# The second MLP of a three-stage kernel in three groups of 768 tokens, one PSUM bank a block, with norm sums in one column, a halved last tile and a wait margin on transfers

## The chip, the core and the metric

One core of a Trainium2 chip runs the whole program in one launch. The metric is device time in microseconds (us), the median of the runs of a kernel. The engines are TensorE (PE in the profile), VectorE (DVE), ScalarE (ACT), GpSimd (POOL) and SyncE (SP), which only issues transfers here.

## The reference

Three stages, in fp32; q, k and v of the attention are fp32, the weights come as float64 and are converted on the chip.

```python
def _attn_ref(q, k, v, phi):               # batch 4, heads 8, seq 576, head_dim 64, n_mem 32
    a = phi - np.max(phi, axis=2, keepdims=True)
    a = np.exp(a)
    a = a / (np.sum(a, axis=2, keepdims=True) + 1e-09)
    k_m = np.einsum('bhsm,bhsd->bhmd', a, k)
    v_m = np.einsum('bhsm,bhsd->bhmd', a, v)
    ...                                     # softmax(scale * q @ k_m.T) @ v_m
def _moe_ref(x, w_in, w_out):              # 2304 tokens, 512 -> 2048 -> 512
    h = x @ w_in
    g = h * (1.0 / (1.0 + np.exp(-1.702 * h)))
    return (g @ w_out).astype(np.float32)
def _moe2_ref(x, w_gate, w_val, w_out, rms_g):   # 2304 tokens, 512 -> 1536 -> 512
    rms = np.sqrt(np.mean(x * x, axis=-1, keepdims=True) + 1e-06)
    xn = x / rms * rms_g
    g = xn @ w_gate
    silu = g * (1.0 / (1.0 + np.exp(-g)))
    val = xn @ w_val
    return (silu * val @ w_out).astype(np.float32)
```

## The kernel before, in words

**Numbers.** A product of fp32 values is made of three matmuls of fp32r parts: each operand is split into a high part (a cast on ACT) and a low part (a subtraction on VectorE or POOL; function `split`), and high x high, low x high and high x low are summed in PSUM.

**Stages.** Attention works by batch and half of the heads; its output feeds the first MLP (steps `a_g1`, `a_g2`), which runs over two pairs of batches, 1152 tokens each, and eight groups of 256 hidden units, and adds into the tiles `x2_0` and `x2_1`. Meanwhile the weights of the second MLP are loaded, converted from float64 (`w_conv c ...`, tiles `raw_c`, `cv`) and put into a DRAM cache.

**The second MLP, the stage of the change.** First RMS norm, by 384 tokens: `norm_1` squares and adds (tiles `sq`, `sr`), `norm_2` sums over the partitions by matmuls against ones into `pnm` and takes the inverse root on columns of 3 (tile `r`), `norm_3` spreads it by transposes (`pnr`, `rb`), `norm_4` scales `x2`. Then gate and value products by a Winograd-like scheme: tokens form two halves, hidden units and inputs two blocks each, and 7 products (weights A11, A12, S1 to S4, A22 against token blocks B11, B21, B22, T1 to T4) stand for 8. The token blocks are made by `t_a` to `t_d` in big tiles `tba`, `tbb`, `tbc`, `tbd`. For each of 12 groups f of 128 hidden units, `s_g3` runs the products (`product`, line 1496) and collects them in tiles `c`, named p, u, v and s: ACT copies a product out of PSUM, VectorE adds the next one to it (`c<-c,ps_S`), ACT applies silu, and the two results are multiplied and split into `pp` tiles. After every second f, `s_g4` multiplies by the output weights (512 columns, PSUM tile `pg4`) and adds into `oacc`; `put` sends finished rows from SP.

The pass runs twice: "b" for the first pair of batches, "s" for the second. In "b" the weight blocks (`s0_f_...`, in the profile `s_A`, `s_S`, `s_o`) are made from the cached weights (`s_weights`, tile `s`, `raw_b_vg`) and written to `cache_s`; "s" reads them back (`s_again`). In "b" also the last conversions and the norm of the second pair are done.

A product here has 576 tokens and takes two PSUM banks, 288 columns in each:

```python
for q in range(2):
    n = slice(q * HALF, q * HALF + HALF)
    for y, z in ((0, 0), (1, 0), (0, 1)):
        for e in range(2):
            PE.matmul(ps[:, 512 * q : 512 * q + HALF], lhsT=a[y][:, e], rhs=b[:, z, e, n], ...)
```

**What orders the work.** Every operation is recorded first (all of them by the helper at line 612) and then ordered by `Plan.order`, a list scheduler with costs for each operation, due times (`dues`), a table that makes steps due earlier (`HASTE`) and a table that moves single operations to another engine (`OTHER`). Where PE would find no work before an operation that takes a new PSUM tile, `fill` puts matmuls on the constant `ones_r` there. Each engine and the SP queue then run their instructions in that fixed order. PSUM is a pool of 4 tiles of two banks each, `big` has 6 tiles, `cv` 5, `w` 10, `gp` 3.

## Time and profile before

| | before |
|---|---|
| median of 3 runs | 834.79 us (833.22 to 837.85) |
| the profiled execution | 838.53 us, of it span 836.8 us |
| PE busy | 820.4 us (98%) |
| VectorE busy | 630.9 us (75%) |
| ACT busy | 439.1 us (52%) |
| POOL busy | 223.2 us (27%) |
| moved by DMA | 166.92 MB, 199 GB/s |
| mean granted clock | 0.996 |

The span is from the first to the last instruction; 1.7 us of the execution lie outside it. Busy shares are over the whole span; since the stages have different limits, the table by stage tells more. In a row, "out<-in xcount" names the tile written and those read (buffer numbers left out), and a "releaser" is what ended a wait. A matmul's own duration overlaps with its neighbours, so the pace is read from starts, not from durations. In the profile tiles are grouped by the first part of their names, so `ps_A` stands for `ps_A11` and `ps_A12`, `pg` also for `pg4`. The second MLP runs from 409 to 832.

### The profile page before, as it was taken

How to read it: one execution, taken by the hardware profiler on the slowest of the kernel's cores; microseconds unless marked ns; L12 is line 12 of the kernel's file. 1: busy time of each engine (PE TensorE's matmuls, PEld its weight loads, DVE VectorE, ACT ScalarE, POOL GpSimd, SP SyncE). 2: the span in 40 equal slices, each digit the busy share in tenths (PEclk: the TensorE clock that was granted, in tenths of full speed). 3: DMA queues.
4: the chain of work that ended last, by engine and by line, in shares of the span. 5: the costliest groups of instructions: out<-in, count | busy, mean ns of one | idle time of the engine just before them, and what ended most of it. 6: DMA issues, size and time to landing. Idle time of an engine off the chain costs nothing.

```text
span 836.8 us, 15257 instructions
## 1 busy us (share of the span) xinstructions
PE 820.4 (98%) x5893; PEld 784.2 (94%) x5893; DVE 630.9 (75%) x1052; ACT 439.1 (52%) x774; POOL 223.2 (27%) x187
## 2 busy tenths in 40 slices
PE   8899999899999999999999999999999999999997
PEld 7799999899999999999999999999999999999996
DVE  7889999799899899899898788576775334445444
ACT  5797766577688565655566545444352332222220
POOL 4533384434542433682511112122000000000000
PEclk9999999999999999999999999999999999999999
DMA  9996756957967975564776579263556452633504
GB/s 340 286 289 159 256 175 214 221 174 260 287 205 225 325 217 191 197 207 152 242 244 226 177 248 333 111 239 122 169 170 193 155 176 73 206 120 108 176 1 113
DMA packets 76759, 166.92 MB, mean 199 GB/s; under 512 B 7312, under 2 KB 29328, under 8 KB 76688
## 3 DMA queue, kind: packets, MB, share of 16 engines
q1 hardware_dynamic: 76688, 165.97, 61.3%
q8 instruction: 46, 0.75, 0.4%
q14 instruction: 25, 0.20, 0.1%
HBM read 106.69 MB, written 59.24 MB: 198 GB/s over the span
## 4 chain that ended last, share of the span: by engine, by line
PE 89%; DVE 3%; DMA 2%; ACT 1%; issue 1%; SPq 0%; DVEq 0%
PE pg L612 50%; PE ps_A L612 23%; PE ps_S L612 9%; PE pq L612 2%; PE pvm L612 2%; DMA stage<-in_v_dram 2%; PE pk L612 1%; DVE pad L612 1%; DVE x L612 1%; PE pnm L612 0%; DVE stage L612 0%; DVE gr L612 0%; PE pnr L612 0%; DVE vm_0l L612 0%; DVE vm_1l L612 0%
## 5 line engine op out<-in xcount | busy, mean ns | idle before, releaser
L612 PE MATMUL pg<-gr,a_outh 128*128 128x384 f32 (+1 forms) x736 | 193.6, 334 | 0.0
L612 PEld LDWEIGHTS pg<-gr,a_outh 128*128 128x128 f32 x736 | 132.8, 188 | 0.6 <-DVE gr L612 0.3
L612 PE MATMUL pg<-gr,a_outl 128*128 128x384 f32 (+1 forms) x368 | 121.9, 331 | 0.0
L612 PE MATMUL pg<-s_o,pp 128*128 128x512 f32 x432 | 112.6, 390 | 0.0
L612 ACT COPY c<-ps_A 128x576 f32<-128x576 f32 x72 | 46.1, 641 | 115.4 <-PE ps_A L612 114.4
L612 PEld LDWEIGHTS pg<-s_o,pp 128*128 128x128 f32 x432 | 79.5, 188 | 15.0
L612 DVE TENSOR_TENSOR x<-x,pg 128x768 f32<-128x768 f32 (+1 forms) x86 | 80.0, 930 | 17.3 <-PE pg L612 16.2
L612 DVE TENSOR_TENSOR oacc<-oacc,pg 128x1024 f32<-128x1024 f32 (+1 forms) x54 | 56.3, 1042 | 47.2 <-PE pg L612 47.0
L612 PE MATMUL ps_A<-tba,s_A 128*128 128x288 f32 x576 | 83.1, 295 | 0.0
L612 PEld LDWEIGHTS ps_A<-tba,s_A 128*128 128x128 f32 x576 | 79.1, 188 | 0.8
L612 POOL TENSOR_TENSOR gr<-gf,gr 128x192 fp32r<-128x192 f32 (+2 forms) x47 | 49.6, 1063 | 88.3 <-ACT gr L612 71.4
L612 DVE TENSOR_TENSOR c<-c,ps_S 128x576 f32<-128x576 f32 x48 | 36.1, 753 | 46.7 <-PE ps_S L612 38.3
L612 PEld LDWEIGHTS pg<-gr,a_outl 128*128 128x128 f32 x368 | 69.3, 188 | 0.0
L612 POOL TENSOR_TENSOR pp<-c,pp 128x576 fp32r<-128x576 f32 (+2 forms) x3 | 4.0, 1346 | 237.5 <-ACT pp L612 237.5
L612 ACT ACTIVATE gf<-pg 128x576 f32<-128x576 f32 x64 | 41.4, 649 | 47.9 <-PE pg L612 41.7
L612 PE MATMUL pg<-s_o,tbd 128*128 128x512 f32 x216 | 60.9, 390 | 0.0
L612 DVE TENSOR_TENSOR c<-c 128x576 f32<-128x576 f32 x44 | 33.3, 756 | 27.8 <-ACT c L612 26.7
L612 ACT CAST gr<-gf 128x576 fp32r<-128x576 f32 (+2 forms) x92 | 45.9, 528 | 4.0 <-PE pg L612 2.3
L612 PEld LDWEIGHTS pg<-s_o,tbd 128*128 128x128 f32 x216 | 39.6, 188 | 7.3
L612 PE MATMUL ps_A<-tbd,s_A 128*128 128x288 f32 x288 | 42.2, 295 | 0.7 <-ACT c L612 0.7
L612 PE MATMUL ps_A<-tbc,s_S 128*128 128x288 f32 x288 | 42.2, 295 | 0.0
L612 PE MATMUL ps_S<-tbb,s_S 128*128 128x288 f32 x288 | 42.1, 295 | 0.0
(238 smaller groups left out, 1818.1 us busy)
## 6 DMA issues: line engine op xcount, KB each, us to landing
cache_s<-s_S SPq DMA_DIRECT2D x24, 512.0 KB, 4.5
s_S<-cache_s SPq DMA_DIRECT2D x24, 512.0 KB, 3.8
cache_b<-cv SPq DMA_DIRECT2D x36, 256.0 KB, 4.9
raw_a_in<-in_moe_w_in_dram SPq DMA_DIRECT2D x16, 512.0 KB, 5.9
raw_a_out<-in_moe_w_out_dram SPq DMA_DIRECT2D x16, 512.0 KB, 5.3
raw_c_gate<-in_moe_w_gate_dram SPq DMA_DIRECT2D x12, 512.0 KB, 5.5
raw_c_val<-in_moe_w_val_dram SPq DMA_DIRECT2D x12, 512.0 KB, 5.4
raw_c_o<-in_moe_w_out_dram SPq DMA_DIRECT2D x12, 512.0 KB, 4.4
```

What stands on the lines that cost most here:

```text
L612: getattr(self.real[op.eng], op.name)(*op.args, **op.kw)
```

## The change

The second MLP runs over three groups of `GT` = 768 tokens (passes "b", "s" and "r") in place of two of 1152; "s" and "r" read the weight blocks back. A block of a product has 384 tokens, so one product is 6 matmuls of 384 columns into one PSUM bank; a tile `ps_a` holds two products in its two banks, `ps_c` one. The tiles `tba` and `tbc` hold three blocks each, `tbb` goes. The norm adds its squares into a tile `sm` and sums by one-column fp32 matmuls, without the split. The last 128 tokens are done in two halves of 256 columns (`s_end`), and the last but largest piece of the last row block is issued by ACT. In the planner, results of SP's transfers count as landed 1 us later (`LAND`), and PE's operations are joined into one unit only where what they need comes before. HASTE and OTHER are new tables of the same form (55 and 186 lines of the diff, most of them left out below).

```diff
+    LAND = 1.0
...
     HASTE = {
-        "a_g1 0 2 0": 233.6,
...
+        "a_g2 1 5 2": 116.4,
...
+        if op.name == "dma_start":
+            return 0.47, 0.0
...
-            if u and u.ops[-1].out.tensor.name == op.out.tensor.name and u.line == op.line:
+            if (u and u.ops[-1].out.tensor.name == op.out.tensor.name and u.line == op.line
+                    and all(of[o].n <= u.n for o in op.after)):
...
-                    ease = self.EASE if u.done > 50 else 0.0
+                    ease = self.EASE + (self.LAND if e == "SP" else 0.0) if u.done > 50 else 0.0
...
+    GT = 768
...
+    TURN = "bsr"
...
-        sm = sq[0][:, :TB]
-        G.tensor_tensor(out=sm, in0=sm, in1=sq[0][:, TB:], op=ALU.add)
-        sr = nrm[pr, t] = gpp.tile([P, 2, 2, TB], F32R, tag="gp", name="sr")[:, 0]
-        A.copy(out=sr[:, 0], in_=sm)
-        sub_lo(G, sr[:, 1], sm, sr[:, 0])
+        sm = nrm[pr, t] = cv("sm")[:, :TB]
+        G.tensor_tensor(out=sm, in0=sq[0][:, :TB], in1=sq[0][:, TB:], op=ALU.add)
...
-            c = slice(s * P, (s + 1) * P)
-            for y in range(2):
-                PE.matmul(
-                    ps[:, c], lhsT=sr[:, y, c], rhs=ones_r, start=(y == 0), stop=(y == 1)
-                )
+            PE.matmul(
+                ps[:, s : s + 1], lhsT=sm[:, s * P : (s + 1) * P], rhs=ones_f, start=True, stop=True
+            )
...
+    def quarter(gi, i, j, e):
+        h, t = divmod(2 * gi + j, NTB)
+        return x2[h][:, 2 * i + e, t * TB : t * TB + TB]
...
-        blocks(pr, "tba", ("B11", "B21"))
+        blocks(pr, "tba", ("B11", "B21", "T1"))
...
-        blocks(pr, "tbb", ("T1", "T2"))
...
-        blocks(pr, "tbc", ("T3", "B22"))
+        blocks(pr, "tbc", ("T2", "T3", "B22"))
...
+            parts.append((ln, to[:, cols], oacc[gi][r0 : r0 + ln, kk, cols]))
             n0 += ln
+        parts.sort(key=lambda x: -x[0])
+        for i, (ln, to, x) in enumerate(parts):
+            (A if last and i else SP).dma_start(out=to, in_=x)
...
+    def product(gi, a, b, f, ps, fresh=True):
+        a, b = wt["s", gi, f][a], tb[gi, b]
+        i = 0
+        for y, z in ((0, 0), (1, 0), (0, 1)):
+            for e in range(2):
+                PE.matmul(
+                    ps, lhsT=a[y][:, e], rhs=b[:, z, e],
+                    start=(fresh and i == 0), stop=(i == 5), skip_group_check=True,
+                )
+                i += 1
...
+            ps = both("ps_a")
+            part["a"], part["b"] = ps[:, :TB], ps[:, 512 : 512 + TB]
+            product(gi, "A11", "B11", f, part["a"])
+            A.copy(out=part["p"], in_=part["a"])
+            x, y = part["p"], psum("ps_c")[:, :TB]
+            product(gi, "A12", "B21", f, y)
+            V.tensor_tensor(out=x, in0=x, in1=y, op=ALU.add)
...
+                split(o, *(to[:, y, j * TB : j * TB + TB] for y in range(2)))
...
+    def s_end(gi, g, kk):
+        for j in range(2):
+            ps = psum("pg4")[:, :256]
...
+            o = oacc[gi][:, kk, c]
+            V.tensor_tensor(out=o, in0=o, in1=ps, op=ALU.add)
+            put(gi, kk, c, j == 1)
...
-            if later and t < 2:
+            if later and key[1] > 4 and t == 1:
...
-    for kk in range(PT // P):
-        line(s_g4, 1, NB - 1, kk, False)
+    for kk in range(GT // P - 1):
+        line(s_g4, 2, NB - 1, kk, False)
+    line(s_end, 2, NB - 1, GT // P - 1)
```

How the order changes is shown at three places. A row is an instruction (or a run of like ones) with the tile written, those read, and the shape; L612 and L632 are the recording helper before and after.

PE, from the end of the first products of the second MLP to the first `pg4` rows (f = 0 and 1; `s0_0_...` are weights of f = 0). Before:

```order
L612 MATMUL ps_S1_824<-tbb0_672,s0_1_S1_787 128x288 x12
L612 MATMUL pnr_803<-ident_90,r_797 128x128 x3
L612 MATMUL ps_A11_809<-tbc0_688,s0_1_S3_788 128x288 x12
L612 MATMUL ps_A11_837<-tba0_659,s0_2_A11_813 128x288 x12
L612 MATMUL ps_A11_809<-tbd0_777,s0_0_A22_751 128x288 x12
L612 MATMUL ps_S1_824<-tbc0_688,s0_1_S3_788 128x288 x12
L612 MATMUL ps_A12_838<-tba0_659,s0_2_A11_813 128x288 x12
L612 MATMUL ps_A11_837<-tbb0_672,s0_2_S1_814 128x288 x12
L612 MATMUL ps_S1_849<-tbb0_672,s0_2_S1_814 128x288 x12
L612 MATMUL pg4_874<-s0_0_o2_761,tbd0_777 128x512 x3
L612 MATMUL pg4_874<-s0_1_o2_800,pp_832 128x512 x3
```

After:

```order
L632 MATMUL ps_a_781<-tbd0_693,s0_0_A22_751 128x384 x6
L632 MATMUL ps_a_781<-tbc0_687,s0_0_S3_752 128x384 x6
L632 MATMUL ps_a_804<-tbc0_687,s0_1_S3_787 128x384 x6
L632 MATMUL ps_c_805<-tba0_659,s0_1_A11_785 128x384 x6
L632 MATMUL ps_a_804<-tbd0_693,s0_0_A22_751 128x384 x6
L632 MATMUL ps_a_804<-tbc0_687,s0_1_S3_787 128x384 x6
L632 MATMUL pnr_797<-ident_90,r_796 128x128 x3
L632 MATMUL ps_a_822<-tba0_659,s0_2_A11_808 128x384 x6
L632 MATMUL ps_c_823<-tba0_659,s0_2_A11_808 128x384 x6
L632 MATMUL pg4_834<-ones_r_92 128x512 x3
L632 MATMUL pg4_834<-ones_r_92 128x128
L632 MATMUL pg4_834<-s0_0_o2_761,pp_799 128x512 x3
```

Products are runs of 6 in place of 12, the two banks of a `ps_a` tile are used in turn, and 4 filler matmuls on `ones_r` stand ahead of the first `pg4` product, which comes after two products of f = 2 (before it came after four).

VectorE at the same place, between the first `ps_c` addition and the `pg4` rows. Before:

```order
L612 TENSOR_TENSOR c_807<-c_807,ps_S1_824 128x576
L612 TENSOR_TENSOR s2_812<-raw_b_2_vg_811 128x256 x2
L612 TENSOR_TENSOR s2_812<-s2_812,raw_b_2_vg_811 128x256
L612 SCALAR_TENSOR_TENSOR cv_802<-raw_c_5_val_1_801,cv_802 128x512
L612 TENSOR_TENSOR s2_812<-raw_b_2_vg_811,s2_812 128x256
L612 SCALAR_TENSOR_TENSOR cv_802<-raw_c_5_val_1_801,cv_802 128x512
L612 TENSOR_TENSOR s0_2_S1_814<-s2_812,s0_2_S1_814 128x512
L612 TENSOR_TENSOR c_806<-c_806,ps_S1_824 128x576
L612 TENSOR_TENSOR c_833<-c_833,ps_A12_838 128x576
L612 TENSOR_TENSOR sq0_1_1_819<-sq0_1_1_819,sq1_1_1_820 128x768
```

After:

```order
L632 TENSOR_TENSOR c_800<-c_800,ps_c_805 128x384
L632 TENSOR_TENSOR pp_799<-c_778,pp_799 128x384
L632 TENSOR_TENSOR pp_799<-c_777,pp_799 128x384
L632 TENSOR_TENSOR c_801<-c_801,ps_a_804 128x384
L632 TENSOR_TENSOR c_800<-c_800,c_803 128x384
L632 SCALAR_TENSOR_TENSOR x2_1_526<-x2_1_526,rg_94,rb_798 128x384
L632 TENSOR_TENSOR c_818<-c_818,ps_c_823 128x384
L632 TENSOR_TENSOR pp_814<-c_800,pp_814 128x384
L632 TENSOR_TENSOR pp_814<-c_801,pp_814 128x384
L632 SCALAR_TENSOR_TENSOR x2_1_526<-x2_1_526,rg_94,rb_798 128x384 x3
```

The collecting steps (`c`, `pp`) are 384 columns wide; the weight steps (`s2`, 256 and 512 columns) and the scaling of `x2_1` keep their widths and stand between fewer columns of products.

SP, the last issues of the program (`oacc` rows to the output). Before:

```order
L612 DMA out_0_dram<-oacc1_1063 96x512
L612 DMA out_0_dram<-oacc1_1063 64x512 x2
L612 DMA out_0_dram<-oacc1_1063 96x512
L612 DMA out_0_dram<-oacc1_1063 32x512 x2
L612 DMA out_0_dram<-oacc1_1063 96x512
L612 DMA out_0_dram<-oacc1_1063 64x512 x2
```

After:

```order
L632 DMA out_0_dram<-oacc2_1186 32x512
L632 DMA out_0_dram<-oacc2_1186 64x512
L632 DMA out_0_dram<-oacc2_1186 96x256
L632 DMA out_0_dram<-oacc2_1186 32x256
L632 DMA out_0_dram<-oacc2_1186 96x256
L632 DMA out_0_dram<-oacc2_1186 64x512
```

The last row block goes in two halves of 256 columns; a 32x256 piece of the second half has left this queue for ACT's, and a 64x512 piece of the block before it now stands last.

## Rows read from the trace of the kernel before

**Rows 1.** The page: busy time by engine; shares of the chain.

```profile
PE 820.4 (98%) x5893; PEld 784.2 (94%) x5893; DVE 630.9 (75%) x1052; ACT 439.1 (52%) x774; POOL 223.2 (27%) x187
...
PE 89%; DVE 3%; DMA 2%; ACT 1%; issue 1%; SPq 0%; DVEq 0%
```

**Rows 2.** By stage: length, busy PE PEld DVE ACT POOL, PEclk, DMA share, GB/s.

```profile
20.00:43.00 23.00, 20.23 (x348) 17.65 (x346) 19.93 (x53) 17.53 (x42) 11.69 (x16) 1.00 1.06 288
125.00:160.00 35.00, 31.56 (x259) 30.82 (x258) 30.51 (x49) 22.49 (x40) 16.48 (x16) 0.98 0.81 215
350.00:405.00 55.00, 55.00 (x360) 55.00 (x359) 51.69 (x69) 30.37 (x53) 32.49 (x25) 1.00 0.55 184
362.00:400.00 38.00, 38.00 (x249) 38.00 (x248) 37.73 (x52) 19.50 (x34) 16.82 (x14) 1.00 0.64 212
405.00:450.00 45.00, 44.29 (x309) 43.37 (x308) 39.95 (x81) 24.94 (x43) 11.83 (x9) 1.00 0.73 237
409.00:611.00 202.00, 201.29 (x1321) 190.15 (x1320) 156.15 (x272) 99.66 (x173) 32.89 (x28) 1.00 0.59 204
484.00:509.00 25.00, 25.00 (x173) 24.01 (x172) 21.79 (x36) 13.68 (x26) 4.22 (x5) 1.00 0.88 315
611.00:832.00 221.00, 221.00 (x1398) 205.69 (x1396) 105.95 (x141) 65.67 (x109) 2.25 (x2) 1.00 0.42 137
```

**Rows 3.** PE's waits: total us, times, longest us.

```profile
PE pk L612 <- DMA stage<-in_v_dram: 2.8, 1, 2.8
```

**Rows 4.** Chain of waits, 400 to 440 and 780 to 837: start, us, what.

```profile
409.23 4.77 PE ps_A L612 x36
...
425.51 0.62 PE pnm L612 x6
...
821.26 10.92 PE pg L612 x48
```

**Rows 5.** Timeline of PE, 341 to 348, first MLP: start, us, what.

```profile
343.22 0.51 PE L612 MATMUL pg<-gr,a_outh 128*128 128x384 f32 x2
...
347.38 0.51 PE L612 MATMUL pg<-gr,a_outh 128*128 128x384 f32 x2
```

**Rows 6.** Timeline of PE at 18 us.

```profile
18.29 0.61 PE L612 MATMUL pk<-ones_f,y 128*128 128x1 f32 x4
18.75 0.36 PE L612 MATMUL pk<-ones_f,stage 128*128 128x1 f32 x2
```

**Rows 7.** Instruction groups of VectorE by shape: busy us, mean ns, idle.

```profile
L612 DVE TENSOR_TENSOR x<-x,pg 128x768 f32<-128x768 f32 x78 | 74.0, 949 | 15.4 <-PE pg L612 14.4
...
L612 DVE SCALAR_TENSOR_TENSOR cv<-raw_c_val,cv 128x512 uint32<-128x512 uint32 x24 | 19.0, 798 | 0.2
...
L612 DVE TENSOR_SCALAR cv<-cv 128x512 uint32<-128x512 uint32 x36 | 18.1, 509 | 0.2
...
L612 DVE TENSOR_TENSOR s_S<-s,s_S 128x512 fp32r<-128x512 f32 x19 | 13.3, 700 | 2.1 <-ACT s_S L612 2.1
...
L612 DVE TENSOR_TENSOR pp<-c,pp 128x384 fp32r<-128x384 f32 x15 | 8.8, 584 | 3.2 <-ACT pp L612 3.2
...
L612 DVE TENSOR_TENSOR s<-raw_b_vg 128x256 f32<-128x256 f32 x20 | 7.8, 418 | 0.0
...
L612 DVE SCALAR_TENSOR_TENSOR r<-r 128x3 f32<-128x3 f32 x36 | 6.1, 169 | 0.4
```

**Rows 8.** The same in 350 to 405; and timeline of VectorE at 111.

```profile
L612 DVE SCALAR_TENSOR_TENSOR cv<-raw_c_o,cv 128x512 uint32<-128x512 uint32 x6 | 6.2, 1025 | 0.1
...
110.99 3.76 DVE L612 TENSOR_SCALAR pad<-pad 128x512 uint32<-128x512 uint32 x1
```

**Rows 9.** Timelines of VectorE and SP, the end.

```profile
832.20 0.69 DVE L612 TENSOR_TENSOR oacc<-oacc,pg 128x512 f32<-128x512 f32 x1 [0.67 <-PE pg L612]
...
832.92 1.11 SPq L612 DMA_DIRECT2D out_dram<-oacc  x2
```

**Rows 10.** Chain of waits, 120 to 165.

```profile
143.42 13.23 DMA stage<-in_v_dram
```

More of the change, by code (lines that the diff above doesn't have):

```diff
@@ L2 @@
 from functools import reduce
-from itertools import islice
+from itertools import chain, islice
 import concourse.bass as bass
@@ L1512, in places @@
-    def places(pr, f):
-        if f % 3 == 0:
-            x = tb[pr, "tbd"][:, 1].rearrange("p y e n -> p y (e n)")
-            return [(0, x)]
-        if f % 3 == 1:
-            x, y = [gpp.tile([P, 2, 2, TB], F32R, tag="gp", name="pp") for i in range(2)]
-            part["rest"] = y[:, 1]
-            return [(0, x.rearrange("p a y n -> p (a y n)").rearrange("p (y n) -> p y n", y=2)), (2 * TB, y[:, 0])]
-        x = gpp.tile([P, 2, 2, TB], F32R, tag="gp", name="pp")
-        return [(0, part["rest"]), (TB, x.rearrange("p a y n -> p (a y n)").rearrange("p (y n) -> p y n", y=2))]
@@ L1552, in s_g3 @@
+            A.activation(out=part["s"], in_=part["a"], func=AF.Silu)
+            product(gi, "S4", "B22", f, part["b"], False)
+            x = part["u"]
+            V.tensor_tensor(out=x, in0=x, in1=part["b"], op=ALU.add)
+            to = pt[gi, f] = place(gi, f)
             for j, (x, y) in enumerate((("p", "s"), ("u", "v"))):
@@ L1772 @@
             do(step)
-    for kk in range(PT // P):
-        line(s_g4, 1, NB - 1, kk, False)
+    for step in late:
+        line(*step)
+    for kk in range(GT // P - 1):
+        line(s_g4, 2, NB - 1, kk, False)
+    line(s_end, 2, NB - 1, GT // P - 1)
     plan.ones, plan.one, plan.pre = ones_r, ones_f, pre
```

426 lines of the change are left out of this document (210 added, 216 removed).

## The prediction

> **What bounds the kernel now.** I read the page first [rows 1]: TensorE (PE) is busy 98% of the span and 89% of the chain that ended last is PE, so time goes when PE has less to do or waits less; 16.4 us of the span are PE's idle time. The table by stage [rows 2] tells where: 2.8 us in 20:43, 3.4 us in 125:160, 0.7 us in 405:450 where the second MLP starts, and nothing in 611:832, where PE is busy 221.00 of 221 us. The granted clock is 1.00 in these stages (0.98 in one), the 2.4 GHz level, and the change gives PE no longer pauses, so I add nothing for the clock. The list of PE's waits [rows 3] names the largest: 2.8 us for one transfer. So the second MLP (409 to 832) is bound by PE's own pace, and what counts is the pace per matmul and whether VectorE (DVE) still keeps up. DVE is busy 156.15 of 202 us in the first half of that MLP and 105.95 of 221 in the second [rows 2].
>
> The profiled execution took 838.53 us, the median of the runs is 834.79, which is 3.7 less. I sum changes against the profile and subtract the sum from the median. About 4.2 us (0.5%) is what a measurement of this kernel can tell from no change.
>
> **Part by part.**
>
> *Products.* Before: 24 times 84 = 2016 matmuls of 288 columns, 36 in 4.77 us [rows 4], 132.5 ns each: 267.1 us. After: 36 times 42 = 1512 of 384 columns. The trace has that shape in the first MLP: from 343.22 to 347.38 there are 24 in 4.16 us [rows 5] (eight times two of these rows and one of a second operand between them), 173.3 ns each: 262.0 us. **-5.1 us**. Columns in all are the same; what goes is 504 times the part of a matmul that does not grow with columns. The rows give that part as 132.5 - 120 = 12.5 ns at 288 columns and, from 48 of 512 in 10.92 us [rows 4], 227.5 - 213.3 = 14.2 ns; with the one or the other at 384 columns the term is -6.3 or -3.7, which are its bounds. The g4 matmuls stay 648 of 512 columns, but for 12 that become 24 of 256: nothing but some 0.1 us.
>
> By the Trainium skill ("TensorE: Matmul & The Clock Gate", Back-to-back issue gap) a warm matmul follows the last after N/2.4 + 2.5 ns. This trace does not agree at 288 or 512 columns (132.5 against 122.5 ns); by the rule the term would be 504 x 2.5 = 1.3 us.
>
> *Norm.* Six times, 6 matmuls of 128 columns (0.62 us [rows 4]) become 3 of one fp32 column. One such instruction of the program stands in the trace as two passes, and 4 passes take 0.46 us (18.29 to 18.75 [rows 6]), 0.115 us each. So 3 cost 6 passes, 0.69 us: **+0.5 us** over six, not a gain (-1.6, if one pass each did, to +0.6). The six casts of sr on ACT and six subtractions go; ACT is busy 24.94 of 45 us in 405:450 [rows 2] and POOL 11.83, so nothing.
>
> *Tail.* The last VectorE addition becomes 256 columns wide: 0.69 us for 512 [rows 9] against some 0.42 for 256 [rows 7], -0.27. But SP now sends five pieces at the end (the order's last excerpt): 64x512, 96x256 and 32x256 stand before the last 96x256, and a 64x512 of the older tile behind it. At 0.56 us an issue (2 in 1.11 us, from 832.92 [rows 9]) the last began at E + 1.3 before, with E the end of PE at 832.2, and begins at E + 1.5 after, with the first of the five at E - 0.7 and four ahead of it. Its size, 64x512, stays, and so its landing. The one piece sent by ACT is made up for by the older one behind. **0** (-0.5 to +0.5).
>
> *The order ahead of the second MLP.* PE's program held 51 filler matmuls of 512 and 14 of 128 columns, now 54 and 12, of which 4 and 6 stand in the second MLP. So 50 and 6 stand early: at 227.5 and some 66 ns (the 128-column part alone, 53 + 13, an estimate from the fixed part above) 11.8 against 12.5 us: **-0.8 us**. The transfer that costs 2.8 us was issued at 143.42 and landed 13.23 us later [rows 10]; SP's order there (raw a_0_6 in, the stage2_1 and stage3_0 loads) is the same after, and the PE work ahead of its reader is the same to 1 us. I keep that wait; bounds -3 to +3, what that wait is worth either way.
>
> *The new planned wait margin, HASTE and OTHER tables* act through the order only; they have no instruction of their own. An ACT issue of one DMA costs nothing there, at the end.
>
> *The first third.* All weight work of the first half (202 us, 33 us on POOL [rows 2]) now stands in a third. A third has 504 x 0.1733 + 216 x 0.2275 = 136.5 us of PE work. From the first ps_c addition on VectorE to the first g4 row I count 33 VectorE instructions: 13 of 384 columns (0.58), 3 of 512 (0.70), 2 of 768 (0.95), 2 scalar_tensor_tensor of 512 (0.80), 1 of 256 (0.42), 1 of 384 (0.6) and 11 of 3 columns (0.17) [rows 7]: 16.1 us. PE's rows over the same stretch, 84 of 384 columns, one norm and one transpose step: 15.6 us. There the planner itself set 3 filler matmuls of 512. The same place before had 30.5 us of PE against 32.9 of VectorE, the deficit carried by work PE had ahead. To the fourth g4 row it is 67.6 against 65.8, to the end of the third 124.3 (225 instructions) against 128.2. So VectorE is at most 1.8 us short and must be busy 97%. Rows 2 show that this can be: in 362:400 VectorE was busy 37.73 of 38 us and PE 38.00. **+1.8 us** (+0.7, the idle time of 405:450, to +6). Transfers are denser: some 41 MB, moved at 204 GB/s, now in 138 us, near 300 GB/s; 484:509 ran at 315 GB/s with PE busy 25.00 of 25 [rows 2]. Nothing, while that holds.
>
> *Second and third groups.* VectorE has about half of PE's time (105.95 of 221 us before). The blocks tba, tbc and tbd of the next group wait for buffers of the last; g4 work of the last group stands between, as at 611, where PE lost nothing. 0.
>
> Sum: -5.1 + 0.5 + 0 - 0.8 + 1.8 = **-3.6 us**: 834.9 against the profile's 838.5, **831.2** against the median.
>
> **Rivals.**
>
> *VectorE is short (same).* Where VectorE's two-input steps run beside POOL, they stretch: scalar_tensor_tensor of 512 took 1.03 us in 350:405 (POOL busy 32 of 55), 0.80 over the span, and one 0.51 us step took 3.76 [rows 2, 7, 8]. POOL's part in the first third is 36 instructions, some 40 us of 138 (29%, from 16%). If VectorE is good for 94% only, as 350:405 was on the whole (51.69 of 55), its 124.3 us need 132.2, 4.0 more than PE's 128.2: -5.1 + 0.5 - 0.8 + 4.0 = -1.4, **833.4**. Against: in 350:405 PE lost nothing. By the Trainium skill ("SBUF — State Buffer", Who interferes with whom) a VectorE instruction with two SBUF inputs and a GpSimd one that reads SBUF shut each other out; the stretched rows agree.
>
> *VectorE is the bound (slower).* Wherever PE waited for VectorE's chains, VectorE itself was only 87% busy: 19.93 of 23 in 20:43, 30.51 of 35 in 125:160 [rows 2], for it waits for ACT's casts and transfers in turn. At 87% its 124.3 us take 142.9, 14.7 more than PE has: -5.4 + 14.7 = +9.3, **844**. It decides from the point where VectorE's share in the first third cannot pass 90% (124.3 of 137.8, 9.6 us late: -5.4 + 9.6 = +4.2); one per cent less is 1.5 us more. For: one PSUM bank a block leaves c = c + ps one 384-column step before the bank is taken again. Against: 362:400.
>
> *The re-laid start wins more (faster).* The stages 20:43 and 125:160 alone hold 6.2 us of PE's idle time [rows 2]. If the margin on transfers puts work ahead of the reader of stage3_0 and the 2.8 us wait goes with 1 to 2 us of others, it is -3.6 - 4.3 = **827**. Against: the order at that place is the same.
>
> *The products save nothing (same).* If a matmul's part that does not grow with columns were so small at 384 columns that 504 of them gave back 1.3 us, -1.3 would replace -5.1: **835.0**. The paces at 288, 384 and 512 columns [rows 4, 5] speak against it. That is the rule named above.
>
> **How the numbers follow.** The forecast (827 to 835) gets 0.45, half of it beyond 4.2 us; VectorE short 0.20; the start 0.19; VectorE the bound 0.13; products 0.03. Faster by over 0.5% (under 830.6): 0.19 + 0.23 = 0.42. Slower (over 839): 0.13. The rest, 0.45, is within. The range takes in the sum with its bounds and the two cases beside it: 823 (the start and the largest products term) to 838 (a first third 6 to 7 us late); it leaves out the bound case and a few in 100 below.
>
> **What would show it.** After: 12 matmuls of 288 in 1.59 us become 6 of 384 in 1.04; pnm x3 takes 0.69 us; a window over the first third with PE idle 1 to 2 us and VectorE 95% or more; the two later thirds with PE idle near 0; the 2.8 us wait for stage still in the list. It is wrong if PE idles over 4 us in the first third, if a 384-column run of 6 takes over 1.06 us, or if PE's idle time ahead of the second MLP changes by more than 4 us.

## The result and the profile after

| | before | after |
|---|---|---|
| median | 834.45 us (833.22 to 837.85, 6 runs) | 840.07 us (838.69 to 843.62, 6 runs) |
| ratio | | 1.0071, 95% interval 1.0043 to 1.0098 |
| the profiled execution | 838.53 us | 838.69 us, of it span 836.6 us |

The change costs **5.6 us**; the forecast was 831.2, with a range from 823 to 838. The two profiles are as long as each other all the same: that of before took longer than any of its runs shown here, that of after is the shortest of its own. So the profiles are compared by stretches here, and totals by the medians.

The page of the changed kernel, busy time by engine and shares of the chain:

```profile
PE 819.7 (98%) x5396; PEld 778.5 (93%) x5396; DVE 627.6 (75%) x1135; ACT 445.6 (53%) x849; POOL 213.3 (25%) x183
...
PE 87%; DVE 8%; DMA 2%; ACT 1%; issue 1%; POOL 1%; DVEq 0%; ACTq 0%
```

PE has 497 instructions less and is as busy as before; VectorE's share of the chain went from 3% [rows 1] to 8%. The table by stretch (columns as in [rows 2]), cut at the first product of each group of the second MLP:

```profile
400.50:546.00 145.50, 142.12 (x759) 131.62 (x758) 124.17 (x248) 84.13 (x170) 42.23 (x38) 1.00 0.82 286
546.00:685.20 139.20, 137.97 (x721) 128.22 (x720) 72.33 (x125) 48.75 (x101) 1.27 (x1) 1.00 0.64 213
685.20:832.00 146.80, 146.19 (x764) 135.35 (x762) 70.16 (x113) 44.65 (x91) 3.48 (x3) 1.00 0.59 196
```

PE idles 3.4 us in the first group, and also in the second (1.2) and third (0.6); the second pass of before lost nothing [rows 2]. VectorE is busy 85% of the first group. PE's waits from 400 us on (engine, tile, releaser: us, times, longest):

```profile
PE ps_a L632 <- DVE c L632: 2.3, 4, 0.6
PE ps_a L632 <- ACT c L632: 1.8, 3, 0.6
PE ps_a L632 <- DVE s_S L632: 0.7, 1, 0.7
PE ps_a L632 <- ACT s_S L632: 0.3, 1, 0.3
```

None of these was in the list of before but one of 0.7 us behind ACT. Of the first line, 0.5 us lie in the first group and 1.8 in the other two. A wait costs more than its idle time, as the last section works out. In the chain of waits twelve matmuls of products take 2.10 us in a row and 2.35 to 2.38 behind a wait; of the difference 0.10 us is the first matmul's, the rest is the length of the last one, to whose end such a piece is counted:

```profile
576.05 2.10 PE ps_a L632 x12
...
595.21 0.50 ACT c L632
...
595.73 0.57 DVE c L632
...
596.32 1.50 DVE c L632 x3
...
597.87 2.35 PE ps_a L632 x12
```

**The account.** Over the second MLP, from PE's starts (a matmul's time is that to the next one's start; "over the pace" is what products and output matmuls take beyond 132.5, 173.3 and 227.5 ns at 288, 384 and 512 columns):

| us | before (two profiles) | after |
|---|---|---|
| first product to the start of the last matmul | 422.7, 423.3 | 431.3 = 145.5 + 139.2 + 146.5 |
| products | 267.1 | 262.0 |
| 12 matmuls of the first MLP, moved behind the first product | 0 | 2.1 |
| filler matmuls | 0 | 1.5 |
| matmuls of the norm, with what they add to the one behind | 3.0, 3.0 | 3.0 |
| over the pace | 1.3, 1.9 | 11.0 = 6.4 + 2.7 + 1.9 |

The norm adds nothing here. With 0.3 for the last tile, whose halves take 12 matmuls of 256 columns in place of 6 of 512, -5.1 + 2.1 + 1.5 + 9.4 + 0.3 = +8.2, which is what the lengths say (8.0 to 8.6). Of the 11.0 us, 11 places of more than 0.12 us hold 7.0: eight in the first group (4.7), two in the second (1.6), one in the third (0.8). With the 2.1 us taken off, as they are only moved, the second MLP is 6.2 us longer.

The parts ahead of it vary from execution to execution in both kernels. The stretch of 35 us that holds the transfer wait [rows 2, 3] in three kernels: after,

```profile
125.00:160.00 35.00, 35.00 (x288) 34.35 (x286) 33.10 (x54) 25.46 (x47) 20.19 (x16) 1.00 0.85 223
```

the kernel before, profiled a second time,

```profile
125.00:160.00 35.00, 33.13 (x257) 32.43 (x256) 30.53 (x49) 22.02 (x40) 16.05 (x14) 0.93 0.85 212
```

and the changed kernel, broken off before the second MLP (an experiment below), with the same instructions up to there:

```profile
125.00:160.00 35.00, 32.45 (x254) 31.61 (x254) 29.00 (x48) 24.18 (x45) 20.20 (x16) 0.92 0.86 222
```

One wait of 0 to 2.8 us for the transfer into `stage`, and a granted clock of 0.92 to 1.00 in this stretch, make much of the difference between reaching the second MLP at 400.5 and past 405. In the profile after the wait was absent. It was 0 to 0.6 us in seven traces of whole kernels with the order of after, which reach the second MLP at 400.5 to 403.2, and 2.6 in the one broken off; with the order of before it was 2.8, 1.9 and 1.8 (broken off). So in most executions seen the changed order does lose that wait.

### The profile page after: what moved, and what is told of

Its sections match the earlier page's. It is cut to its first block, busy times and chain, and to the rows that moved or that the text cites. A ratio compares the mean times of both kernels' runs of the same rounds, so it can differ in the third digit from the quotient of the medians.

```text
span 836.6 us, 14554 instructions
## 1 busy us (share of the span) xinstructions
PE 819.7 (98%) x5396; PEld 778.5 (93%) x5396; DVE 627.6 (75%) x1135; ACT 445.6 (53%) x849; POOL 213.3 (25%) x183
## 4 chain that ended last, share of the span: by engine, by line
PE 87%; DVE 8%; DMA 2%; ACT 1%; issue 1%; POOL 1%; DVEq 0%; ACTq 0%
PE pg L632 50%; PE ps_a L632 26%; PE ps_c L632 4%; PE pq L632 3%; PE pvm L632 2%; PE pk L632 2%; DVE pad L632 2%; DMA kmisc<-in_phi_dram 1%; DVE c L632 1%; DVE x L632 1%; DVE stage L632 1%; ACT c L632 0%; DMA raw_a_in<-in_moe_w_in_dram 0%; PE pnm L632 0%; DVE kmisc L632 0%
## 5 line engine op out<-in xcount | busy, mean ns | idle before, releaser
L632 PE MATMUL pg<-gr,a_outh 128*128 128x384 f32 (+1 forms) x736 | 194.4, 334 | 0.1
L632 PEld LDWEIGHTS pg<-gr,a_outh 128*128 128x128 f32 x736 | 132.9, 188 | 0.3 <-PE pk L632 0.2
L632 PE MATMUL ps_a<-tbc,s_S 128*128 128x384 f32 x648 | 127.8, 336 | 2.8 <-ACT c L632 1.8
L632 PE MATMUL pg<-gr,a_outl 128*128 128x384 f32 (+1 forms) x368 | 122.0, 332 | 0.0
L632 PEld LDWEIGHTS ps_a<-tbc,s_S 128*128 128x128 f32 x648 | 114.0, 188 | 6.1 <-ACT c L632 2.8
L632 ACT COPY c<-ps_a 128x384 f32<-128x384 f32 x108 | 51.6, 479 | 125.9 <-PE ps_a L632 124.7
L632 PE MATMUL pg<-s_o,pp 128*128 128x512 f32 (+1 forms) x438 | 108.7, 389 | 0.0
L632 PEld LDWEIGHTS pg<-s_o,pp 128*128 128x128 f32 x438 | 81.0, 188 | 15.6
L632 DVE TENSOR_TENSOR c<-c,ps_a 128x384 f32<-128x384 f32 x72 | 39.7, 552 | 73.8 <-ACT c L632 66.5
L632 DVE TENSOR_TENSOR oacc<-oacc,pg 128x1024 f32<-128x1024 f32 (+2 forms) x49 | 55.4, 1131 | 50.2 <-PE pg L632 50.2
L632 DVE TENSOR_TENSOR x<-x,pg 128x768 f32<-128x768 f32 (+1 forms) x86 | 79.9, 930 | 16.8 <-PE pg L632 15.6
L632 POOL TENSOR_TENSOR c<-c 128x384 f32<-128x384 f32 x7 | 8.0, 1137 | 274.9 <-issue 248.4
L632 PEld LDWEIGHTS pg<-gr,a_outl 128*128 128x128 f32 x368 | 69.2, 188 | 0.0
L632 ACT ACTIVATE gf<-pg 128x576 f32<-128x576 f32 x64 | 41.6, 650 | 47.1 <-PE pg L632 42.5
L632 POOL TENSOR_TENSOR gr<-gf,gr 128x192 fp32r<-128x192 f32 (+2 forms) x35 | 40.0, 1146 | 79.4 <-ACT gr L632 60.6
L632 PE MATMUL pg<-s_o,tbd 128*128 128x512 f32 x216 | 56.7, 392 | 0.0
L632 PEld LDWEIGHTS pg<-s_o,tbd 128*128 128x128 f32 x216 | 40.3, 188 | 7.9
L632 ACT ACTIVATE c<-ps_a 128x384 f32<-128x384 f32 x36 | 17.7, 491 | 56.2 <-PE ps_a L632 52.0
L632 PE MATMUL ps_a<-tbd,s_A 128*128 128x384 f32 x216 | 44.5, 340 | 2.4 <-DVE c L632 2.3
L632 ACT CAST gr<-gf 128x576 fp32r<-128x576 f32 (+2 forms) x92 | 45.7, 526 | 1.6
L632 PE MATMUL ps_a<-tba,s_A 128*128 128x384 f32 x216 | 44.0, 338 | 0.0
L632 POOL TENSOR_SCALAR cv<-cv 128x512 f32<-128x512 f32 x19 | 38.3, 2016 | 21.1 <-ACT cv L632 13.9
```

The source lines that it names most:

```text
L632: getattr(self.real[op.eng], op.name)(*op.args, **op.kw)
```

## The experiments

Rows of experiments can have other line numbers for the recording helper (such as L633 to L635), since their text is a few lines longer.

**The kernel before, once more.**

> The kernel before, profiled a second time. The summed stages gave a difference of about -3.6 us against the first profile (838.5), yet the changed kernel lost 5.6 us against the median (834.5). Theory: the first profile holds some 4 us of waits ahead of the second MLP that most executions do not have; then this profile is near 834 to 835, with PE idle in the first 160 us near 7 us in place of 11, and the second MLP again takes 422 to 423 us. Rival: the first profile is typical; then it is near 838 again, with the 2.8 us wait for a transfer still there.

837.77 us; the wait for the transfer was 1.9 us, in place of 2.8, the first product started at 407.68 in place of 409.07, and the first wait behind ACT in the second MLP was 1.3 in place of 0.7. The second MLP took 423.3 us. The theory's 834 to 835 did not come; the wait stayed in the main, as the rival had it. Both profiles of before are over 3 us longer than its median, and the part of them that repeats is the second MLP. So the loss of after lies in the second MLP; the stages ahead scatter.

### Dependences taken away one at a time, order kept

The operations are recorded and ordered as in the changed kernel, so that every engine's order stays word for word; only at issue is an operand replaced.

```diff
-                getattr(self.real[op.eng], op.name)(*op.args, **op.kw)
+                getattr(self.real[op.eng], op.name)(*op.args, **{**op.kw, **op.swap})
...
             product(gi, "S2", "T2", f, part["a"], False)
             A.copy(out=part["u"], in_=part["a"])
+            plan.ops[-1].swap = dict(in_=ones_f.to_broadcast([P, TB]))
...
             A.copy(out=x, in_=part["a"])
+            plan.ops[-1].swap = dict(in_=ones_f.to_broadcast([P, TB]))
             V.tensor_tensor(out=x, in0=x, in1=part["b"], op=ALU.add)
+            plan.ops[-1].swap = dict(in1=ones_f.to_broadcast([P, TB]))
```

g1 has the first of the three added lines, g2 the last, g3 all three.

> The changed kernel with every engine's order kept word for word; ScalarE's copy of the S2 block (u) reads a constant tile instead of the PSUM bank, so the S3 product into that bank has no copy to wait for. The copy itself stays on ScalarE with its size; the result of the S2 block is lost. Theory chain (the time goes in product, copy, product of one f): the four waits of 0.73 to 0.85 us ahead of S3 in the first group (3.2 us together) go, the first group's 145.5 us become 142 to 143, the other groups stay at 139.2 and 146.5, the time falls from 840.1 to about 837. Theory weights (in the first group a block has to wait for its weights from VectorE anyway): the waits move to the next product or to the weights, the first group stays at 145 or more and the time at 840.

> The changed kernel with every engine's order kept word for word; VectorE's addition v + b reads a constant tile in place of the second bank of ps_a, so the A22 product, which writes the first bank of that tile, no longer waits for VectorE, as its waits in the program show (Activation in place of DVE). The addition stays in place with its size; the S1 block is left out of v. Theory tie: the waits of 0.78 us at A22 in groups 2 and 3 (three) go and those of the first group shrink (1.0 us together), so groups 2 and 3 fall from 139.2 and 146.5 to 137.7 and 145.7, the first from 145.5 to about 144.5, the time from 840.1 to about 837. Theory weights: the first group stays at 145 or more; groups 2 and 3 fall as said, the time is 838.

> Both together, and the copy of v reads the constant tile too: from S2 to A22 no product into ps_a waits for what an engine reads out of it; orders word for word as in the changed kernel, sizes too; the S2, S3 and S1 blocks are left out of the result. Theory chain and tie: the waits between the blocks of one f are what the second MLP lost, so the three groups go to about 141, 137.5 and 145 us (423.5 to 424.5 in place of 431.3), near what pace and fillers alone give with the small waits left, and the time to about 833, near the 831.2 forecast. Theory weights: the first group stays at 144 us or more, since S weights then end the waits; the time stays over 836.

| | median | ratio to before | groups | over the pace |
|---|---|---|---|---|
| after | 840.07 | 1.0071 [1.0043, 1.0098] | 145.5, 139.2, 146.5 | 6.4, 2.7, 1.9 |
| g1, copy | 839.65 | 1.0055 [1.0038, 1.0072] | 145.6, 139.2, 146.5 | 6.5, 2.8, 1.9 |
| g2, tie | 836.83 | 1.0028 [1.0015, 1.0041] | 143.9, 137.4, 145.6 | 4.8, 0.9, 1.0 |
| g3, both | 835.72 | 1.0012 [0.9998, 1.0027] | 143.6, 137.4, 145.6 | 4.5, 0.9, 1.0 |

**The tie is shown.** A22 accumulates into the first bank of `ps_a`; VectorE's addition v + b reads the second. They never touch the same bank, but they are one tile, and 34 waits of A22 products in the built program of after are for VectorE (17 for it alone, 17 with a transfer too). In g2 nearly all are for ACT. The first A22 product of after, and of before, with the semaphores that the built programs make it wait for:

```
1698 L632 MATMUL ps_a_781<-tbd0_693,s0_0_A22_751 128x384 [waits DVE_49]
1701 L612 MATMUL ps_A11_782<-tbd0_777,s0_0_A22_751 128x288 [waits Activation_49]
```

In the kernel before the two blocks lay in tiles of their own (`ps_A11`, `ps_S1`), and A22 waited for ACT's copy alone. What the wait looks like in the third group, timeline of PE after:

```profile
712.31 1.21 PE L632 MATMUL ps_c<-tba,s_A 128*128 128x384 f32 x6
714.12 1.32 PE L632 MATMUL ps_a<-tbd,s_A 128*128 128x384 f32 x6 [0.61 <-DVE c L632]
715.29 1.21 PE L632 MATMUL ps_a<-tbc,s_S 128*128 128x384 f32 x6
```

and what VectorE does meanwhile:

```profile
711.99 0.55 DVE L632 TENSOR_TENSOR c<-c,ps_a 128x384 f32<-128x384 f32 x1 [3.49 <-ACT c L632]
712.58 1.03 DVE L632 TENSOR_TENSOR c<-c 128x384 f32<-128x384 f32 x2
713.52 0.55 DVE L632 TENSOR_TENSOR c<-c,ps_a 128x384 f32<-128x384 f32 x1
```

VectorE waits 3.49 us itself, so it is far from busy; but in its order the addition that A22 waits for stands behind another addition and two multiplications, and ends at 714.07, 0.05 us before A22 starts. The same place in g2:

```profile
711.14 1.20 PE L633 MATMUL ps_c<-tba,s_A 128*128 128x384 f32 x6
712.18 1.20 PE L633 MATMUL ps_a<-tbd,s_A 128*128 128x384 f32 x6
713.22 1.20 PE L633 MATMUL ps_a<-tbc,s_S 128*128 128x384 f32 x6
```

1.81 us between the starts of `ps_c` and A22 have become 1.04. The gain is not that of a faster VectorE: the addition that reads the constant takes 0.62 us, where it took 0.55. Groups 2 and 3 lose every place over 0.12 us and fall by 1.8 and 0.9 us, the first by 1.6: **4.3 us by the lengths**, 3.2 by the medians, as the theory of the tie had it (its numbers for the second and third groups were 137.7 and 145.7).

By the Trainium skill ("Perfetto Trace Analysis", Optimizing Tensor Performance) independent matmul groups should rotate through different PSUM banks, so that reading one out overlaps the next group. The trace agrees only in part: here the banks did differ, and the reading still held the next product back, since the program's waits go by tile.

**The copy alone is refuted.** In after, S3 waits for ACT's copy of the block before it in the same bank:

```profile
434.85 1.20 PE L632 MATMUL ps_a<-tba,s_S 128*128 128x384 f32 x6
436.68 1.32 PE L632 MATMUL ps_a<-tbc,s_S 128*128 128x384 f32 x6 [0.62 <-ACT c L632]
```

In g1 that wait is gone, and two products later A22 waits 0.75 us for VectorE:

```profile
438.05 1.20 PE L633 MATMUL ps_a<-tbc,s_S 128*128 128x384 f32 x6
439.10 1.20 PE L633 MATMUL ps_a<-tba,s_A 128*128 128x384 f32 x6
...
441.61 1.14 PE L633 MATMUL ps_a<-tbd,s_A 128*128 128x384 f32 x5 [0.75 <-DVE c L633]
```

so the first group keeps 145.6. With both away 143.6 are left, 4.5 over the pace, and the waits are those for weight blocks, its list from 400 us on:

```profile
PE ps_a L633 <- DVE s_S L633: 0.9, 2, 0.7
PE ps_a L633 <- DVE s_A L633: 0.3, 1, 0.3
PE ps_a L633 <- ACT s_S L633: 0.3, 1, 0.3
PE pg L633 <- DVE pp L633: 0.3, 1, 0.3
```

The outcome lies between the two theories: the later groups came to the 137.5 and 145 that the first named, the first group to 143.6 in place of 141, and the time (835.7) just under the 836 of the other. What is left in the first group are mostly waits for weights. No run took those away by themselves; that several chains end close behind one another there, so that taking one away shows the next, is read from g1 and g3.

### The tie taken away with the result whole

```diff
-            x, y = part["p"], psum("ps_c")[:, :TB]
+            ps = both("ps_c")
+            count[0] += 1
+            part["d"] = part["b"] if count[0] in OLD else ps[:, 512 : 512 + TB]
+            x, y = part["p"], ps[:, :TB]
...
             product(gi, "S1", "T1", f, part["b"])
+            for o in plan.ops[-6:]:
+                o.swap = dict(ps=part["d"])
```

(the same for S4, and `in1=part["d"]` for the two additions that read the block.)

> The changed kernel with every engine's order kept word for word, nothing left out: in 28 of the 36 steps of f the blocks S1 and S4 go into the second bank of the tile ps_c instead of that of ps_a, so that what VectorE reads there no longer holds the A22 product into ps_a; the other 8 (f = 1, 5 and 11 of the first group, 1, 7 and 10 of the second, 5 and 7 of the third) stay as they are, since five PSUM tiles would be needed at once there. S1 now has to wait for the addition of ps_c. Theory tie: what the run without the tie gained (1.6 us in the first group, 1.8 in the second, 0.9 in the third; 3.2 us by the medians) comes back as far as its waits fall on the 28, 2 to 3 us of it, and the time is 837 to 838. Rival: the new wait of S1 for the addition of ps_c takes the place of the one removed, since that addition comes only one product earlier; then the time stays at 840 and the list of PE's waits shows ps_c behind VectorE.

A miss on both sides: 850.68 us, 1.0173 [1.0127, 1.0218]. Group lengths 144.9, 149.3 and 148.0; the first fell by 0.6, the others rose by 10.1 and 1.5. The largest of PE's waits from 400 us on, in this run:

```profile
PE pg L635 <- ACT oacc L635: 3.8, 1, 3.8
PE ps_a L635 <- DVE oacc L635: 1.8, 2, 1.3
PE pg L635 <- DVE c L635: 1.4, 2, 0.7
```

They are waits for a PSUM tile: `pg` and `ps_a` cannot start before an older tile has been read out into `oacc`. `ps_c` is now held to the end of its f, and the pool has four tiles; the order had been made for one that is free after one addition. S1's new wait was small (0.2 to 0.4 us at three places). So the tie is cheap to remove only where PSUM has a tile to spare. A pool of one-bank tiles, with an order made for it, was not tried.

### Two tiles with the order made anew, and the weight sums left out

> The changed kernel, but blocks a and b of a group f in two PSUM tiles in place of the two banks of one. Theory (one tile ties two banks): in the changed kernel every A22 product waits for VectorE's addition of block b, and ACT's copy of the S2 block for the S1 product behind it; with two tiles A22 waits for ACT alone, and the stalls of the second and third group (4.6 us above pace) fall under 1.5 us. The first group has fewer tiles to spare and more fillers in the order (about 34 of 512 columns against 4), so it may lose 5 us or more: total 838 to 845. Rival (VectorE is short of time): the second and third group keep their stalls, since VectorE's work there is the same.

> The changed kernel, but the planner treats the two banks of a PSUM tile as one when it orders (no instruction added, only another order; about 23 fillers of 512 columns in the first group). Theory of the tie: the order now has other PE work where the tie makes PE wait; stalls above pace in the second and third group fall from 4.6 to under 1.5 us, the first group loses 5 to 6 us in fillers as it did in stalls: total 835 to 838. Rival (VectorE is short of time): nothing falls in the later groups, total 839 to 843.

> The changed kernel without the four sums and differences of weights that make the S blocks (48 steps of 256 columns, about 20 us of VectorE and POOL in the first group); the S weights are the value weights instead. Theory (VectorE is short of time in the first group): the first group's 6.4 us above pace fall to under 2 us, the later groups stay at 4.6: total 835 to 836.5. Rival (the tie alone): the first group keeps 4 us or more, total 838 to 840.

```diff
-            ps = both("ps_a")
-            part["a"], part["b"] = ps[:, :TB], ps[:, 512 : 512 + TB]
+            part["a"] = psum("ps_a")[:, :TB]
...
+            part["b"] = psum("ps_b")[:, :TB]
```

Above e1. In e2 the planner treats a PSUM tile as a whole (`q, m, write = 15, 3, True`); in e3 the sums are left out (`for i, x in enumerate((v, v, g2, v))`).

| | median | ratio | groups |
|---|---|---|---|
| e1, two tiles | 845.1 | 1.0126 [1.0110, 1.0143] | 150.1, 139.2, 145.5 |
| e2, planned tie | 853.51 | 1.0226 [1.0207, 1.0245] | 158.1, 138.9, 147.9 |
| e3, no weight sums | 841.21 | 1.0078 [1.0059, 1.0097] | 144.6, 139.2, 146.5 |

In e1 the third group lost its wait; its last two stretches:

```profile
553.60:692.80 139.20, 137.90 (x722) 128.19 (x721) 74.10 (x125) 48.72 (x103) 1.02 (x1) 1.00 0.66 225
692.80:838.60 145.80, 145.80 (x764) 135.33 (x762) 71.50 (x116) 45.80 (x95) 3.40 (x3) 1.00 0.57 191
```

PE is busy 145.80 of 145.80. But the first group grew by 4.5 us, with 7.9 us of fillers in place of 1.5: so most of the loss is the new order's. All three missed: e1 took 0.1 us more than its 838 to 845, and its later groups kept some 3.5 us over the pace in place of under 1.5 (the second waits 1.3 us for `tbc`); e2 was forecast at 835 to 838 or 839 to 843; e3 at 835 to 836.5 or 838 to 840. In e1 and e2 the new order hides the price of the tie; that is why the runs above keep the order. e3, some 20 us of VectorE and POOL lighter, has a first group of 144.6, so the group does not stand or fall with the sums.

### VectorE's own time, order kept

> The changed kernel with its order kept word for word on every engine, but the four weight sums of an f work on 8 columns in place of 256 (some 38 VectorE steps of 0.42 us and 10 POOL steps of 0.74 become tiny; the S weights are then ones). The earlier edits all re-made the order, and orders made anew by tables meant for another kernel lose 5 to 27 us by themselves; this one does not. Theory (VectorE has too little time in the first group): its 6.4 us above pace fall to 2.5 or less, total 835 to 837. Rival (each f waits on its own chain of product, copy, product, and on the order, however fast VectorE is): 5 us or more stay, total 838.5 to 840.

> The changed kernel with its order kept, but every weight sum that VectorE makes is made twice (some 38 steps of 0.42 us more, 16 us, the results the same). Theory (VectorE has too little time in the first group): nearly all of it lengthens the first group, 8 to 16 us, total 848 to 856. Rival (chains and order, VectorE with time to spare): less than 4 us, total 840 to 844.

```diff
+        for o in plan.ops[-4:]:
+            o.swap = {x: o.kw[x][:, :8] for x in ("out", "in0", "in1")}
```

Above f1 (and the S blocks are split from ones); f2 issues the same four sums twice where they stand on VectorE. f1: 840.06 us, 1.0068 [1.0047, 1.0089]. f2: 859.72, 1.0303 [1.0278, 1.0329]. The first group in f1,

```profile
403.20:547.70 144.50, 141.74 (x759) 131.63 (x758) 113.51 (x248) 83.74 (x170) 36.58 (x38) 1.00 0.82 288
```

and in f2:

```profile
401.70:564.60 162.90, 146.59 (x760) 134.47 (x759) 141.18 (x285) 84.80 (x170) 41.84 (x38) 0.98 0.74 256
```

10.7 us less of VectorE's work give back 1.0 us, 17.0 us more cost 17.4. PE's waits in f1's first group:

```profile
PE ps_a L633 <- ACT c L633: 1.8, 3, 0.6
PE ps_a L633 <- DVE s_S L633: 0.7, 1, 0.7
```

After has these two in its first group, 0.3 behind ACT for `s_S`, and one for VectorE's addition:

```profile
PE ps_a L632 <- DVE c L632: 0.5, 1, 0.5
```

So with VectorE at 79% only the smaller waits went; the copies and the S weights kept theirs, and 5.4 of the 6.4 us over the pace stay, as the rival said. VectorE's sum of work is not what after loses by. The S weights are late by VectorE's order, as far as one trace shows it: f1 comes to these sums at 452.12, after 2.20 us of scaling `x2_1`, and makes two of them in 0.24 us (0.76 in after, behind the same 2.20); the wait stays 0.7.

f2 went the other way: it lies above the 848 to 856 of the theory that f1 refutes, and far from its rival's 840 to 844. The two go together if VectorE's time runs out between them: its 141.2 us in f2 are more than the 139.1 (145.5 - 6.4) that PE's rows take there without waits, its 124.2 in after are less. And about 3.3 of the 17.4 us are the clock's, an estimate from two stretches of 4.00 us with PE busy throughout at a granted clock of 0.60 and 0.57 (last section). So f2 shows that VectorE has little to spare in the first group; it does not price what after loses.

### Parts of the change put on the kernel before

> The kernel before with the norm sums in one fp32 column as the only edit (two groups of 1152 stay, orders made anew by the same tables). By the sum: 0.69 in place of 0.61 to 0.62 us a norm step, +0.5 us, 834.5 to 836. Rival (one pass a matmul, and six casts and six subtractions fewer give VectorE and ACT room): 832 to 833.5.

> The kernel before with the halved last tile and the ACT issue as the only edit. By the sum: 0 (834 to 835). Rival: the last addition is 0.27 us shorter and the last issue comes 0.5 us earlier, 833.5 to 834.

> The kernel before with everything of the change but the regrouping and the new tables: norm column, halved last tile, the wait margin on SP's transfers, the rule for joining PE's operations. Theory (the loss is made by the groups of 768: waits on chains of ACT and VectorE in the second MLP): within 1.5 us of before, 834 to 836. Rival (the margin and the new order of the early stages make it): 838 or more.

> The changed kernel with the margin on SP's transfers set to 0, tables as they are. Theory (the groups make the loss): 838 to 842, second MLP again 429 to 432 us. Rival (the margin makes it): 836 or less.

| | median | ratio |
|---|---|---|
| p_norm, norm sums in one column | 840.23 | 1.0063 [1.0036, 1.0090] |
| p_tail, last tile in two halves | 834.18 | 0.9993 [0.9976, 1.0011] |
| p_all, all but groups and tables | 846.73 | 1.0132 [1.0108, 1.0156] |
| a_land0, the change with `LAND = 0.0` | 866.9 | 1.0370 [1.0342, 1.0397] |

p_tail settles its part: nothing, as forecast. The other three make the order anew with tables that belong to another kernel and miss their theories' ranges by 4 to 25 us; p_all alone came out on its rival's side, a_land0 and p_norm on neither. The largest wait of p_all is 3.4 us, for attention's tile `pq` behind ACT, a place that the edit does not touch. Their totals say nothing of the norm's 0.5 us or of the margin, and what the margin does ahead of the second MLP stays open. By stretches p_all says one thing: its first product comes only at 416.7, but its second MLP, in two groups and with all else of the change but the tables, takes 424.5 us against 422.7 and 423.3. So, as far as an order made anew can tell, no more than 2 us of the loss there come without the groups and the tables made for them.

### The parts ahead of the second MLP, by themselves

> The kernel before, broken off in front of the first product of the second MLP: every engine keeps its program word for word up to that place and has nothing behind it, so the second MLP and the writes of the output are left out. Its profiled execution should reach the end of TensorE's work near 409 us, as the two profiles of before did (409.07 and 407.68 at the first product), and the run should take 411 to 414 us in all. What it is for is the pair with the changed kernel, broken off at the same place. Theory 1: the parts ahead of the second MLP are as far apart in timed executions as in the profiled ones; then the medians of the pair are 7.2 to 8.6 us apart. Theory 2: only the profiled executions of before are 3 to 4 us long there, and a timed one gains 0.8 by the changed order and 2.1 by the 12 matmuls that moved behind the first product; then the pair is about 3 us apart.

> The changed kernel, broken off in front of its first product of the second MLP in the same way (second MLP and writes left out; 12 matmuls of the first MLP that stand behind that product are left out with it). Theory 1: the median is 7.2 to 8.6 us below that of the kernel before, broken off (as 400.49 stands to 407.68 and 409.07 in the profiles). Theory 2: about 3 us below it (0.8 of the order, 2.1 of the 12 matmuls), with a profiled execution that is again 7 us or more below the other's.

```diff
             for _, _, op in self.order():
+                if op.eng == "PE" and op.kw.get("lhsT") is not None and getattr(op, "step", "").startswith("s_g3"):
+                    break
```

cut_before 407.99 us (405.24 to 409.11, 4 runs), cut_after 408.93 (407.98 to 410.10, 4 runs). After PE's last matmul 1.0 us of span followed in the one (406.3 of 407.3) and 2.7 in the other (405.6 of 408.3), so by PE's end after is earlier by 1.7 - 0.9 = 0.8 us, of which 2.1 are matmuls left out. Theory 1 (7.2 to 8.6) is refuted: most of the 8.6 us between the two full profiles at the first product were the luck of two executions. Theory 2 (about 3) is nearer, but was not met either. The broken-off kernel does not stand for the whole one: its profiled execution waited 2.6 us for `stage` and ended PE's work at 405.6, where seven traces of whole kernels with the same order got there at 400.5 to 403.2. With that, and a scatter of 2 to 4 us within each kernel, the size of the term stays open.

## Why the prediction was wrong

- **Products, -5.1: right.** 6 matmuls of 384 columns take 1.04 us in the chain (12 in 2.08 to 2.10), 173.3 ns each. The rival that the products save nothing falls with it.
- **Norm, +0.5: about 0.1.** The six passes take 0.56 us, and 0.13 more lie on the product after them, 0.69 together as the prediction had it:

```profile
413.16 2.08 PE ps_a L632 x12
415.24 0.56 PE pnm L632 x6
415.80 2.21 PE ps_a L632 x12
```

But it set this against the 0.62 of before alone [rows 4], where the product after it is longer too, by 0.04 to 0.06 (12 matmuls in a row take 1.58 to 1.60):

```profile
426.13 1.64 PE ps_S L612 x12
```

By PE's starts the two are the same in the second MLP.

- **Tail, 0: right.** The last addition and ACT's issue behind it in after stand as the sum had them, and p_tail timed the part at 0.9993:

```profile
832.06 0.42 DVE L632 TENSOR_TENSOR oacc<-oacc,pg 128x256 f32<-128x256 f32 x1 [0.29 <-PE pg L632]
832.51 0.38 ACTq L632 DMA_DIRECT2D out_dram<-oacc  x1
```

- **The order ahead, -0.8 (3 either way): not refuted.** The medians leave 5.6 - 8.2 = -2.6 for it with the 2.1 us that moved, so -0.5; the broken-off pair gives +1.3 (2.1 - 0.8), and stands for the whole kernel badly.
- **The first third, +1.8: wrong, the step that failed.** It measured 6.4 us over the pace and 1.5 of fillers, against 1.3 to 1.9 and none before. That is some 6.3 us in place of 1.8. VectorE's sum was right (124.2 us, 124.3 counted), and the denser transfers cost nothing (286 GB/s, and no wait of PE for a transfer in the list). The step compared VectorE's sum of durations with PE's, and asked whether one is longer. f1 shows that it is not a matter of sums: with VectorE at 79%, 5.4 of the 6.4 us stay. What the step left out are single chains: the way from a product through ACT's copy and VectorE's addition back to a product on the same tile, with only as much PE work beside it as the next block of 1.04 us, where it was 1.59 before. g2 and g3 price it: the tie is 1.6 us, the copies 0.3 more. 4.5 us stay; 2.8 of them are waits of over 0.12 us, mostly for weights that come just in time. That share is read from the trace of g3 and was not tested by itself, and the 1.7 below 0.12 us a place stay open.
- **Second and third groups, 0: wrong.** They lost 4.6 us over the pace, 2.7 of them by the tie, which g2 took away. The prediction looked at buffers of token blocks and at VectorE's share (half of PE's time), not at what a product into a tile with two blocks waits for. The diff showed it: one `ps_a` with two parts, read by two engines. What is left of the loss is 0.9 and 1.0 us, about half of it PE's pace at 512 columns (12 in 2.76 us, [rows 4] has 48 in 10.92, which is 2.73); why that rose isn't known. The first third alone would have left the time near 836 (831.2 + 4.5), inside the range; with these two groups it passed 838.
- **The base.** Terms were summed against a profile of 838.5 us and taken off a median 3.7 below it. The long execution's extra time lay ahead of the second MLP, so no term of the second MLP was touched by it, and the account above closes on the medians: -3.6 became +5.6 by 9.4 - 1.8 = 7.6 us of waits and 1.5 of fillers.

The rival that VectorE would be **the bound** gave 844, on the right side and in the right group, and VectorE was indeed at 85% there. Its mechanism, too little of VectorE's time, is refuted for this kernel by f1 (at 87% f1's 113.5 us take 130.5, less than PE has, and the loss stays); it fits f2, where 141.2 at 87% are 162.3 and the group took 162.9. It said nothing of the other two groups. "VectorE is short" (833.4) falls with it (and of its two stretched rows, the one of 3.76 us is a step with one tensor input, so no case of the two-input steps that it speaks of). Of the re-laid start, the wait of 2.8 us did go in most traces, but the medians show no such gain.

The signs that the prediction set show how little PE's idle time tells: it idled 3.4 us in the first third, under the 4 that were to refute the forecast, while its starts show 6.4 over the pace. What it had expected to see and did not come were VectorE at 95% or more there (85%) and idle time near 0 in the later groups (1.2 and 0.6).

## What to carry to other kernels

Sums of busy time tell whether an engine can keep up, not whether it will be in time: when blocks get shorter, list for each product what must have been read out of its tile, in the order of the reading engine, and compare that chain with the PE work that lies beside it. Where a product must not wait for the reading of another block, give the two blocks PSUM tiles of their own, not two banks of one; that tie cost 4.3 us by the lengths here (3.2 by the medians), and neither of the two ways tried (e1, h1) had it back with four tiles in the pool. To price one dependence, keep every engine's order and take that dependence alone away; in five runs an order made anew moved the time by more (5 to 27 us) than what was to be measured.

## What the runs showed of the hardware

A wait of PE costs some 0.27 us more than the idle time shown. At 597.87 in after the starts of two matmuls are 0.95 us apart in place of 0.17, so 0.78 us are lost, of which the profile shows 0.61 as idle, since it counts from the end of the matmul before (0.34 us after its start). The first matmul after the wait then takes 0.28 us to the next start in place of 0.17; so do the first ones behind all nine waits of over 0.15 us in the second MLP (0.28 each). The wait of 0.61 us above set the next product back by 0.77 (1.81 against 1.04 us between starts) in the same way.

In f2 longer pauses of PE were followed by a lower clock. PE was busy 0.71 of 4.00 us and then ran 4 us at a granted clock of 0.60, near the lower of its two levels (1.2 of 2.4 GHz), before it rose to 0.97; after 1.38 of 4.00 us busy (508 to 512) it ran at 0.57:

```profile
456.00:460.00 4.00, 0.71 (x3) 0.39 (x3) 3.93 (x9) 2.36 (x6) 0.46 (x1) 1.00 0.02 6
460.00:464.00 4.00, 4.00 (x14) 3.71 (x15) 3.97 (x7) 2.90 (x5) 1.31 (x1) 0.60 0.82 273
464.00:468.00 4.00, 4.00 (x23) 3.56 (x22) 3.90 (x8) 1.12 (x3) 1.05 (x2) 0.97 0.93 330
...
512.00:516.00 4.00, 4.00 (x16) 4.00 (x15) 0.70 (x1) 1.13 (x3) 1.86 (x2) 0.57 0.86 329
```

The waits of 0.6 us in the changed kernel's second MLP left it at 1.00 in all three groups.
